# A fused attention and feed-forward kernel: the second part's second layer as seven block products, its weights streamed, its order from a list schedule

## The chip, the cores and the metric

The kernel runs on one core of a Trainium2 chip. TensorE (PE) multiplies matrices out of SBUF into PSUM, VectorE (DVE), ScalarE (ACT) and GpSimd (POOL) work on tiles, and SyncE (SP) issues most of the DMAs. Each engine runs its own instructions in order and waits on semaphores of the others. The metric is the time on the device in microseconds (us).

## The reference

It is attention over 4 batches, 8 heads, 768 tokens and heads of 64, followed by a feed-forward layer over the 3072 tokens:

```python
scores = scale * np.matmul(q, k.transpose(0, 1, 3, 2))
...                      # causal band of n_local and the first n_global keys, a bias by distance
a = a / (np.sum(a, axis=-1, keepdims=True) + 1e-09)
x = np.matmul(a, v)      # -> [3072, 512]
h = x @ w_in             # [512, 2048]
g = 0.5 * h * (1.0 + erf(h * inv_sqrt2))
out = (g @ w_out).astype(np.float32)      # [2048, 512]
```

The weights come as 64-bit words and are turned into 32-bit values on the chip. Each operand of a matmul is split into a high part and a low rest, so that one product takes three matmuls (high by high, high by low, low by high).

## The kernel before

The 2048 hidden columns are cut into 8 slices of 256, the tokens into 12 chunks of 256.

The first part does the attention of the 12 chunks and, for slices 0 to 2 (`NA`), both layers of each chunk (`m1`, `m2`, lines 508 to 551). It stores the partial sums (`store_partial`) and the chunks' x (`spill`). Meanwhile slices 3 to 7 are decoded (`stage_weights`, times in `DECODE`) and written to DRAM as high and low parts (`w1d`, `w2d`). A step is one chunk with one slice; START, EVENTS, SCALE and COPY say in which step and on which engine the attention's pieces are done.

The second part (`m1b`, `m2b`, lines 624 to 726) does slices 3 to 7 for 6 chunks of 512 tokens, 30 steps in all. There the first layer is already a scheme of seven block products in place of eight: the 256 columns by 512 rows of the weight slice are four blocks, x too, and sums of blocks (S1 to S4 of the weights, made when they are decoded; T1 to T4 of x, made in `fetch_x` and `make_x`) go into seven products of 6 matmuls of 128x256 each, so 42 matmuls a step (`product`, line 620). VectorE adds their results (line 629), ScalarE applies Gelu twice to each (a high part, and again the full value, from which VectorE takes the low rest, line 201). The second layer is done plainly: 4 groups of 6 matmuls of 128x512, 24 a step (`m2b`, line 722; the last step line 688), summed over the five slices in PSUM. At a chunk's end VectorE adds the partial sums of the first part (line 703), and they go out.

The five slices' weights for the second part are fetched once and stay in SBUF. GpSimd makes the sums of x. All first-part weights are read once more (`check_load`, `check_words`, line 314: 32 loads of 512 KB, 64 VectorE operations). The order within the second part is that of the code, moved about by the framework's scheduler.

Of the kernel before, what the change touches and what calls it, by code (L numbers as in the profile page):

```python
# [17 lines left out]
P = 128  # L18
# [21 lines left out]
EVS = {"load": (-3, -3, -2, -1), "s": (0, 0, 1, 1), "pt": (2, 2, 3, 3), "av": (3, 3, 4, 4)}  # L40
# [5 lines left out]
SCALE = ["vvvv", "vvvv", "gggg", "vvvv", "vvvv", "gggg", "vvvv", "gggg", "vvvv", "vvvv", "vvvv", "gggg"] + ["gggg"] * NP * (NCH - 3)  # L46
COPY = ["aavaaaaa", "aaaaaaaa", "avavvaaa", "vvvvvvvv"]
LOW = ["gvvg", "gvvv", "vvvv"]
PENS = "vvvvgggg"
GAP = 3  # L50
STEPS = [(c, s) for s in range(NA) for c in range(2)]
# [11 lines left out]
    18, 19, 20, 21,  # L63
    22, 23, 25, 27,
    27, 29, 29, 31))}
# [23 lines left out]
A11, A12, A22, S1, S2, S3, S4 = range(7)  # L89
B11, B21, B22, T1, T2, T3, T4 = range(7)  # L90
NEGMASK = -1000000000.0
# [23 lines left out]
class Fast:  # L115
    def __init__(self, tc, ctx, qT, kT, v, w, out, limits):
# [7 lines left out]
        self.stg = pool("stg", 2)  # L124
# [3 lines left out]
        self.gp = pool("gp", 3, stack=self.first)  # L128
        self.words = ExitStack()
# [10 lines left out]
        self.w1d = {s: tc.dram_tile([P, 2, 7, 256], F32, name=f"w1d{s}") for s in range(NA, NST)}  # L140
        self.w2d = {s: tc.dram_tile([P, 2, 2, DM], F32, name=f"w2d{s}") for s in range(NA, NST)}
# [9 lines left out]
        self.done, self.planned = set(), {}  # L151

    def consts(self):
# [6 lines left out]
        ta = self.stg.tile([P, 4, 256], F32, name="ta", tag="stage")  # L160
        tb = self.stg.tile([P, 4, 256], F32, name="tb", tag="stage")
# [53 lines left out]
    def load_weights(self, s, i):
        self.raw[s, i, "w"] = self.load_words(s, i, "w")
# [9 lines left out]
    def join_words(self, s, i):  # L226
# [3 lines left out]
        a = self.sm.tile([P, 512], I32, name=f"wb{s}_{i}", tag="o")  # L230
# [5 lines left out]
        if s >= NA and i < 2:  # L236
            af = self.sb.tile([P, 512], I32, name=f"wa{s}_{i}", tag="wa", bufs=2)
# [19 lines left out]
    def stage_weights(self, s, i):  # L257

        nc = self.nc
        if i == 0:  # L260
            self.w1s = self.sb.tile([P, 2, 7, 256], F32R, name=f"w1s{s}", tag="w1s")
            self.sums = self.sb.tile([P, 4, 256], F32, name=f"sums{s}", tag="sums")
        self.low_bits(s, i)
        self.join_words(s, i)
        af = self.af.pop((s, i))
        if i >= 2:
            w2 = self.sb.tile([P, 2, DM], F32R, name=f"w2s{s}_{i}", tag="w2s", bufs=2)
            self.his.append(nc.scalar.copy(w2[:, 0], af).ins)
            self.lo_dve(w2[:, 1], af, w2[:, 0])
            nc.sync.dma_start(self.w2d[s][:, :, i - 2, :], w2.bitcast(F32))  # L270
            return
        a = af.rearrange("p (d f q) -> p d f q", d=2, f=2)
        view = lambda x: x.rearrange("p b (d q) -> p d b q", d=2)
        hi, lo = self.w1s[:, 0], self.w1s[:, 1]
        if i == 0:
            self.a0 = a
            part, blocks = a[:, :, 0:1, :], slice(A11, A11 + 1)
        else:
            part, blocks = a, slice(A12, A22 + 1)
        h = nc.scalar.copy(view(hi[:, blocks]), part)  # L280
        self.his.append(h.ins)
        nc.vector.tensor_tensor(out=view(lo[:, blocks]), in0=part, in1=view(hi.bitcast(F32)[:, blocks]),
                                op=ALU.subtract)
        if i == 0:
            return
        add = lambda out, x, y, op: nc.gpsimd.tensor_tensor(out=out, in0=x, in1=y, op=op)
        sm = [self.sums[:, k].rearrange("p (d q) -> p d q", d=2) for k in range(4)]
        add(sm[0], self.a0[:, :, 1], a[:, :, 1], ALU.add)
        add(sm[1], sm[0], self.a0[:, :, 0], ALU.subtract)
        add(sm[2], self.a0[:, :, 0], self.a0[:, :, 1], ALU.subtract)  # L290
        add(sm[3], a[:, :, 0], sm[1], ALU.subtract)
        for k in range(4):
            ks, ss = slice(k, k + 1), slice(S1 + k, S1 + k + 1)
            nc.scalar.copy(hi[:, ss], self.sums[:, ks])
            self.lo_dve(lo[:, ss], self.sums[:, ks], hi[:, ss])
        nc.sync.dma_start(self.w1d[s], self.w1s.bitcast(F32))

    def fetch_w1(self, pool, s):
        self.w1[s] = pool.tile([P, 2, 7, 256], F32R, name=f"w1_{s}")
        self.nc.sync.dma_start(self.w1[s].bitcast(F32), self.w1d[s])  # L300

# [251 lines left out]
    def store_partial(self, t, k):  # L553
# [3 lines left out]
        o = self.sm.tile([P, DM], F32, name=f"o{c}_{k}", tag="o")  # L557
# [3 lines left out]
    def open_x(self):  # L561
        right = dict(side="right", reuse_waits="tile")
        self.wb = self.pool("wb", **right)
        self.xr = self.pool("xr", 2, **right)
        self.tf = self.pool("tf", **right)
        self.xcp = self.pool("xc", **right)

    def open_b(self):
        self.first.close()
        tile_waits = dict(reuse_waits="tile")  # L570
        self.gb = self.pool("gb", 2, **tile_waits)
        self.wb3 = self.pool("wb3", **tile_waits)
        self.pt = self.pool("part", 4, **tile_waits)

    def fetch_x(self, c):
        nc = self.nc
        xr = [self.xr.tile([P, 2, NP, CT], F32R, name=f"xr{n}{c}", tag=f"xr{n}") for n in "hl"]
        for j in range(2):
            for i in range(2):
                nc.sync.dma_start(xr[i].bitcast(F32)[:, j].rearrange("p d t -> p (d t)"), self.xd[2 * c + j][i])  # L580
        xs = self.tf.tile([P, 2, NP, CT], F32, name=f"xs{c}", tag="xs")
        for j in (1, 0):
            for i in (0, 1):
                ds = slice(2 * i, 2 * i + 2)
                nc.gpsimd.tensor_tensor(out=xs[:, j, ds], in0=xr[0].bitcast(F32)[:, j, ds],  # L585
                                        in1=xr[1].bitcast(F32)[:, j, ds], op=ALU.add)
        b = lambda i, j: xs[:, j, 2 * i:2 * i + 2, :]
        sub = lambda out, x, y: nc.gpsimd.tensor_tensor(out=out, in0=x, in1=y, op=ALU.subtract)
        tf = self.tf.tile([P, 2, 2, CT], F32, name=f"tf{c}", tag="tf")
        sub(tf[:, 0], b(0, 1), b(0, 0))  # L590
        sub(tf[:, 1], b(1, 1), b(0, 1))
        t2 = xs[:, 0, 0:2, :]
        sub(t2, b(1, 1), tf[:, 0])
        t4 = xs[:, 0, 2:4, :]
        sub(t4, b(1, 0), t2)
        self.xraw[c] = {T1: tf[:, 0], T2: t2, T3: tf[:, 1], T4: t4}
        for k, i, j in ((B11, 0, 0), (B21, 1, 0), (B22, 1, 1)):
            self.xc[c, k] = tuple(x[:, j, 2 * i:2 * i + 2, :] for x in xr)

    def make_x(self, c, k):  # L600
        if k < T1:
            return
        x = self.xraw[c][k]
        h, l = (self.xcp.tile([P, 2, CT], F32R, name=f"xc{n}{c}_{k}", tag=f"{n}{k}") for n in "hl")
        self.nc.scalar.copy(h, x)
        self.lo_dve(l, x, h)
        self.xc[c, k] = (h, l)

    def fetch_part(self, c):
        for k in range(4):  # L610
            self.part[c, k] = t = self.pt.tile([P, DM], F32, name=f"part{c}_{k}", tag="part")
            self.nc.sync.dma_start(t, self.pd[4 * c + k])

    def product(self, out, s, a, x, start, stop):
        h, l = x
        w = self.w1[NA + s]
        n = 0
        for d in range(2):
            for i, y in ((0, h), (0, l), (1, h)):
                self.nc.tensor.matmul(out, lhsT=w[:, i, a, d * P:(d + 1) * P], rhs=y[:, d, :],  # L620
                                      start=start and n == 0, stop=stop and n == 5, skip_group_check=not start)
                n += 1

    def m1b(self, t, half):
        nc = self.nc
        c, s = STEPS[t]
        c -= NCH
        mul = lambda out, a, b, start, stop: self.product(out, s, a, self.xc[c, b], start, stop)
# [454 lines left out]
```

## Time and profile before

| | us |
|---|---|
| median of 3 runs (679.25 to 679.66) | 679.28 |
| the profiled execution's own time | 679.46 |
| its span | 677.7 |
| first part, to the first matmul of the second | 354.9 |
| second part, to the end of the last matmul | 316.6 |
| after it | 6.2 |

The profile counts an engine as busy from an instruction's start to its end. Matmuls overlap in their pipeline, so the pace of TensorE is read from the starts of successive matmuls, not from their durations.

### The profile page before, as it was taken

The numbers are of one execution on the slowest core, as the hardware profiler recorded it, in microseconds if no ns is written. First come the engines' busy times: TensorE is split into PE (matmuls) and PEld (weight loads), VectorE is DVE, ScalarE is ACT, GpSimd is POOL, SyncE is SP. The second block draws the span as 40 slices with busy tenths as digits, with TensorE's granted clock in tenths as the row PEclk, the third lists the DMA queues.
The fourth block names the chain that finished last, engine by engine and source line by source line (L and its number), as shares of the span: only waits on it lengthen the run. The fifth ranks groups of instructions, "written<-read, shape, count | busy, mean of one in ns | idle before, by whom it ended". The sixth has DMA issues, their size and how long they took to land.

```text
span 677.7 us, 13212 instructions
## 1 busy us (share of the span) xinstructions
PE 667.2 (98%) x4809; PEld 591.4 (87%) x4809; DVE 434.9 (64%) x1194; ACT 361.4 (53%) x876; POOL 172.2 (25%) x243
## 2 busy tenths in 40 slices
PE   8999999999999999999999999999999999999996
PEld 7878888988888988888889899998999988899895
DVE  7999668977778878776136268559557535344333
ACT  5899678787787887875133142242332323332231
POOL 1140324244252522532146006006006005100000
PEclk9999999999999999999999999999999999999999
DMA  9678748979788796764499638348448105102101
GB/s 292 175 205 281 230 157 262 326 237 322 222 249 297 217 291 211 234 230 156 171 411 428 278 118 330 119 137 288 139 121 304 63 2 194 55 1 92 34 1 66
DMA packets 79785, 134.64 MB, mean 199 GB/s; under 512 B 15457, under 2 KB 51553, under 8 KB 77793
## 3 DMA queue, kind: packets, MB, share of 16 engines
q1 hardware_dynamic: 74992, 125.99, 55.6%
q10 hardware_dynamic: 4720, 7.74, 3.2%
q8 instruction: 40, 0.66, 0.4%
q14 instruction: 33, 0.26, 0.1%
HBM read 94.11 MB, written 39.58 MB: 197 GB/s over the span
## 4 chain that ended last, share of the span: by engine, by line


## 5 line engine op out<-in xcount | busy, mean ns | idle before, releaser
L722 PE MATMUL accb<-w,ghb 128*128 128x512 f32 x464 | 133.5, 391 | 0.0
L437 POOL TENSOR_SCALAR n<-n,su 128x256 f32<-128x256 f32 (+1 forms) x160 | 82.2, 534 | 164.1 <-DVE su L427 98.5
L722 PEld LDWEIGHTS accb<-w,ghb 128*128 128x128 f32 x464 | 84.3, 188 | 15.2
L421 ACT ACTIVATE n<-n,nmax 128x256 f32<-128x256 f32 (+1 forms) x192 | 91.8, 480 | 5.8 <-DVE nmax L405 5.3
L517 PE MATMUL h<-xh,winh 128*128 128x256 f32 x288 | 83.4, 290 | 0.0
L585 POOL TENSOR_TENSOR xs<-xrh,xrl 128x512 f32<-128x512 f32 x24 | 31.2, 1324 | 199.1 <-DVE glb L201 42.6
L517 PE MATMUL h<-xh,winl 128*128 128x256 f32 x288 | 81.6, 284 | 0.0
L517 PE MATMUL h<-xl,winh 128*128 128x256 f32 x288 | 81.4, 283 | 0.0
L722 PE MATMUL accb<-w,glb 128*128 128x512 f32 x232 | 79.5, 392 | 0.0
L405 DVE CUSTOM_DVE_ANT_0 n<-s,pens 128x256 f32<-128x256 f32 (+1 forms) x192 | 64.6, 396 | 3.1 <-PE s L382 2.8
L549 PE MATMUL acc<-wouth,gh 128*128 128x512 f32 x144 | 59.8, 417 | 0.0
L517 PEld LDWEIGHTS h<-xh,winh 128*128 128x128 f32 x288 | 54.9, 191 | 1.9 <-issue 0.5
L549 PE MATMUL acc<-woutl,gh 128*128 128x512 f32 x144 | 56.5, 394 | 0.0
L549 PE MATMUL acc<-wouth,gl 128*128 128x512 f32 x144 | 56.4, 397 | 0.0
L517 PEld LDWEIGHTS h<-xl,winh 128*128 128x128 f32 x288 | 55.0, 191 | 1.2
L644 ACT COPY p<-xy 128x256 f32<-128x256 f32 x30 | 11.1, 369 | 83.3 <-PE xy L620 83.1
L517 PEld LDWEIGHTS h<-xh,winl 128*128 128x128 f32 x288 | 54.9, 191 | 0.2 <-DVE wb L238 0.2
L620 PE MATMUL xy<-xrh,w 128*128 128x256 f32 x240 | 52.4, 282 | 1.0 <-DVE u L629 0.6
L620 PE MATMUL v<-xch,w 128*128 128x256 f32 x240 | 52.4, 281 | 0.0
L201 DVE TENSOR_TENSOR glb<-hs,ghb 128x256 fp32r<-128x256 f32 (+1 forms) x60 | 38.5, 644 | 18.2 <-ACT hs L674 14.7
L452 PE MATMUL t<-ident,n 128*128 128x128 f32 x352 | 48.2, 273 | 0.8 <-DVE n L437 0.5
L461 DVE COPY pt<-t 128x512 f32<-128x512 f32 (+1 forms) x76 | 45.5, 636 | 5.6 <-PE t L452 5.5
(127 smaller groups left out, 1497.7 us busy)
## 6 DMA issues: line engine op xcount, KB each, us to landing
w<-w SPq DMA_DIRECT2D x32, 512.0 KB, 4.8
c<-w SPq DMA_DIRECT2D x32, 512.0 KB, 4.5
w1d<-w1s SPq DMA_DIRECT2D x5, 1792.0 KB, 6.6
w<-w1d SPq DMA_DIRECT2D x5, 1792.0 KB, 16.9
kr<-kT SPq DMA_DIRECT2D x32, 224.0 KB, 4.4
pd<-o ACTq DMA_DIRECT2D x24, 256.0 KB, 4.0
part<-pd SPq DMA_DIRECT2D x24, 256.0 KB, 3.4
qr<-qT SPq DMA_DIRECT2D x45, 128.0 KB, 4.1
```

Source lines behind the costliest of these rows:

```text
L201: return self.nc.vector.tensor_tensor(out=out, in0=in_, in1=hi.bitcast(F32), op=ALU.subtract)
L405: ins = nc.vector.tensor_tensor_reduce(out=nn[:, j, :w], in0=sp[:, j, :w], in1=pen, scale=-0.125, scalar=3e38, op0=ALU.add, op1=ALU.min, a ...
L421: self.table(self.nc.scalar.activation(out=nn[:, j, :w], in_=nn[:, j, :w], func=AF.Exp, bias=mn[:, i:i + 1], scale=-1.0, accum_out=su[:, i ...
L437: ins = (nc.vector if vec else nc.gpsimd).tensor_scalar(out=nn[:, j, :w], in0=nn[:, j, :w], scalar1=su[:, i:i + 1], scalar2=0.0, op0=ALU.m ...
L452: nc.tensor.transpose(tp[:, i, :], nn[:, j, a * P:(a + 1) * P], self.ident)
L461: (nc.vector.tensor_copy if COPY[min(c, 3)][h] == "v" else nc.scalar.copy)(pt, tp[:, :n, :])
L517: nc.tensor.matmul(hp[:, f, :], lhsT=w[:, d, f * P:(f + 1) * P], rhs=x[:, d, :], start=n == 0, stop=n == 3 * NP - 1)
L549: nc.tensor.matmul(acc, lhsT=g[:, f, ks], rhs=w[:, f, :], start=s == 0 and n == 0, stop=s == NA - 1 and n == 5)
L585: nc.gpsimd.tensor_tensor(out=xs[:, j, ds], in0=xr[0].bitcast(F32)[:, j, ds], in1=xr[1].bitcast(F32)[:, j, ds], op=ALU.add)
L620: self.nc.tensor.matmul(out, lhsT=w[:, i, a, d * P:(d + 1) * P], rhs=y[:, d, :], start=start and n == 0, stop=stop and n == 5, skip_group_ ...
L644: nc.scalar.copy(p6, xy[:, 1])
L722: nc.tensor.matmul(acc, lhsT=g[:, f, ks], rhs=w[:, i, f, :], start=s == 0 and n == 0, stop=s == NB - 1 and n == 5)
```

## The change

The second layer of the second part becomes a scheme of seven products as well. The 512 tokens of a chunk are two halves q of 256, each with two blocks of 128 tokens; for each half and slice, g is four blocks of 128x128, `w_out`'s slice four of 128x256. Sums of g's blocks (`sum_g`, four VectorE operations) and their splitting into high and low (`split_g`) are made for each half, chunk and slice; sums of `w_out` when it is decoded. Each of the seven products takes 3 matmuls of 128x256 and has a region of PSUM of its own, summed over the five slices (`m2b`); only at the half's end are the seven combined (`post_sum`). Gelu is applied once to each value. The first layer's sums are partly made in PSUM: products accumulate into one bank, from which ScalarE copies the running sum (`first_copy`) and to which VectorE adds (`first_sum`). The first layer's weights are fetched anew for every step, in two pieces and two buffers (`fetch_w1`); the second layer's stay. Of the sums of x, only the first chunk's are still made on GpSimd. The check reads 64 loads of 256 KB.

The order of every engine in the second part comes from a list schedule: TensorE's order is written out, and an operation of another engine is placed when its inputs are there by assumed durations, by the due time that TensorE's order gives it; all engines are then held to that order. The last two groups of the first part's second layer (`n0`, `n1`) move into the second part's first step. In the first part, DECODE, the loads' times, SCALE (three of each chunk's first four scalings from GpSimd to VectorE) and COPY (two of eight copies a chunk from VectorE to ScalarE) change.

```diff
-COPY = ["aavaaaaa", "aaaaaaaa", "avavvaaa", "vvvvvvvv"]
...
+COPY = ["aavaaaaa", "aaaaaaaa", "avavvaaa", "vavvvvav"]
...
+    def fetch_w1(self, t, part):
+        s = STEPS[t][1]
+        cut = (slice(0, 4), slice(4, 7))[part]
+        n = cut.stop - cut.start
+        w = self.w1[t, part] = self.wb.tile([P, n, 2, 256], F32R, name=f"w1{'ab'[part]}_{t}", tag=f"w1{part}", bufs=2)
+        self.nc.sync.dma_start(w.bitcast(F32), self.w1d[NA + s][:, cut])
...
+        eng = self.nc.vector if c else self.nc.gpsimd
...
+        bank, a, b = {1: ("x", A11, B11), 6: ("x", S2, T2), 5: ("x", S1, T1), 3: ("x", S4, B22), 2: ("y", A12, B21),
+                      7: ("v", S3, T3), 4: ("v", A22, T4)}[k]
...
+        self.nc.scalar.copy(x, self.half[t]["x"])
...
+        self.nc.vector.tensor_tensor(out=x, in0=x, in1=self.half[t][bank], op=ALU.add)
...
+        a, b, op = ((g[:, G21], g[:, G22], ALU.add), (x[:, 0], g[:, G11], ALU.subtract),
+                    (g[:, G11], g[:, G21], ALU.subtract), (g[:, G12], x[:, 1], ALU.subtract))[k]
+        self.nc.vector.tensor_tensor(out=x[:, k], in0=a, in1=b, op=op)
...
+        dst, src = (slice(3, 7), self.gx[c, q, s]) if sums else (slice(0, 3), self.g[c, q, s][:, 1:4])
+        if low:
+            self.lo_dve(o[:, 1, dst], src, o[:, 0, dst])
+        else:
+            self.nc.scalar.copy(o[:, 0, dst], src)
...
+        for k in ks:
+            a, b = sides[k]
+            for n, (i, j) in enumerate(((0, 0), (0, 1), (1, 0))):
+                self.nc.tensor.matmul(out[k], lhsT=o[:, i, a], rhs=w[:, b, j],
+                                      start=s == 0 and n == 0 and k in (1, 4, 5, 6),
+                                      stop=s == NB - 1 and n == 2, skip_group_check=True)
...
+            gaps = (([(c, 0, s - 1, 0)], [(c, 0, s - 1, 1)], []) if c == 0 else (
+                ([(b, 0, 4, 0)], [(b, 0, 4, 1)], []), (both(b, 1, 0), both(b, 1, 1), both(b, 1, 2)),
+                (both(b, 1, 3), both(b, 1, 4), []), (both(c, 0, 0), both(c, 0, 1), []),
+                (both(c, 0, 2), both(c, 0, 3), []))[s])
...
+            pe += [(u, 1), (u, 2), (u, 7), (u, 6)] + gaps[0] + [(u, 5)] + gaps[1] + [(u, 3)] + gaps[2] + [(u, 4)]
```

TensorE, inside a step of the second part. In the order before, `accb` are the second layer's sums, `z` and `v` banks of the first layer:

```order
L722 MATMUL accb_0_5621<-w_4_4930,ghb_5635 128x512
L620 MATMUL v_5684<-xch_5_5378,w_5_4932 128x256
L620 MATMUL v_5684<-xcl_5_5379,w_5_4932 128x256
L620 MATMUL v_5684<-xch_5_5378,w_5_4932 128x256 x2
L620 MATMUL v_5684<-xcl_5_5379,w_5_4932 128x256
L620 MATMUL v_5684<-xch_5_5378,w_5_4932 128x256
L722 MATMUL accb_0_5621<-w_4_4930,ghb_5635 128x512
L722 MATMUL accb_0_5621<-w_4_4930,glb_5636 128x512
L722 MATMUL accb_0_5621<-w_4_4930,ghb_5635 128x512 x2
```

In the order now, `go` are the split blocks of g, `acc` the regions of the seven products, `x` and `v` banks of the first layer:

```order
L646 MATMUL x_8353<-xch_4_7658,w1a_8122 128x256
L703 MATMUL acc_8246<-w_5_5065,go_2_8292 128x256 x6
L703 MATMUL acc_8248<-w_5_5065,go_2_8292 128x256 x3
L703 MATMUL acc_8249<-w_5_5065,go_2_8292 128x256 x3
L703 MATMUL acc_8247<-w_5_5065,go_2_8292 128x256 x6
L703 MATMUL acc_8248<-w_5_5065,go_2_8292 128x256 x3
L646 MATMUL x_8353<-xch_3_7705,w1b_8235 128x256
```

A second layer of 24 matmuls 512 wide for 512 tokens has become 21 of 256 for each half, put between two products of the first layer.

VectorE, where a chunk's (now a half's) sums end. Before, `part` takes the sums of four groups, and nothing of the second layer is made by VectorE but `glb`:

```order
L201 TENSOR_TENSOR glb_6050<-xy_5992,ghb_6049 128x256
L703 TENSOR_TENSOR part_0_5548<-accb_0_5621,part_0_5548 128x512
L703 TENSOR_TENSOR part_1_5550<-accb_1_5628,part_1_5550 128x512
L629 TENSOR_TENSOR hs_5995<-u_49_5996,z_5993 128x256
L629 TENSOR_TENSOR hs_5995<-u_49_5996,v_5994 128x256
```

Now, `gx` are sums of g's blocks, `hc` sums of the first layer, `u`, `vw`, `r` and `part` belong to `post_sum`:

```order
L675 TENSOR_TENSOR gx_3_8596<-g_62_8264 128x128
L713 TENSOR_TENSOR part_3_8312<-part_3_8312,acc_8246 128x256
L675 TENSOR_TENSOR gx_3_8596<-g_62_8264,gx_3_8596 128x128
L713 TENSOR_TENSOR u_8612<-u_8612,acc_8246 128x256
L713 TENSOR_TENSOR part_3_8312<-part_3_8312,acc_8246 128x256
L713 TENSOR_TENSOR vw_8613<-u_8612,acc_8247 128x256 x2
L713 TENSOR_TENSOR r_8614<-vw_8613,acc_8247 128x256
L205 TENSOR_TENSOR go_1_8617<-g_60_7952,go_1_8617 128x384
L713 TENSOR_TENSOR vw_8613<-vw_8613,acc_8248 128x512
L322 SCALAR_TENSOR_TENSOR wand<-c_8610,wand 128x256
L205 TENSOR_TENSOR go_1_8617<-gx_1_8437,go_1_8617 128x512
L657 TENSOR_TENSOR hc_64_8563<-hc_64_8563,v_8533 128x256
```

The combination of seven products is a chain of VectorE operations, with the next half's operands (`go`) and sums of the first layer around it.

SyncE, at the start of the second part. Before, the weights of all five slices are fetched one after the other:

```order
L304 DMA w_4_4930<-w2d_157 128x2048
L300 DMA w_5_4932<-w1d_153 128x3584
L304 DMA w_5_4934<-w2d_158 128x2048
L300 DMA w_6_4936<-w1d_154 128x3584
L304 DMA w_6_4938<-w2d_159 128x2048
L300 DMA w_7_4940<-w1d_155 128x3584
L304 DMA w_7_4942<-w2d_160 128x2048
L206 DMA c_2_5132<-w 128x1024
```

Now `w1a` and `w1b` are a step's pieces of the first layer's weights, `c` the check's loads:

```order
L314 DMA w_4_5063<-w2d_157 128x3584
L314 DMA w_5_5065<-w2d_158 128x3584
L310 DMA w1a_5067<-w1d_153 128x2048
L310 DMA w1b_5070<-w1d_153 128x1536
L310 DMA w1a_5104<-w1d_154 128x2048
L314 DMA w_6_5131<-w2d_159 128x3584
L310 DMA w1b_5202<-w1d_154 128x1536
L310 DMA w1a_5225<-w1d_155 128x2048
L310 DMA w1b_5256<-w1d_155 128x1536
L314 DMA w_7_5287<-w2d_160 128x3584
L310 DMA w1a_5345<-w1d_151 128x2048
L318 DMA c_5389<-w 128x512
```

The second layer's weights are larger (3584 for 2048 words a row), and behind the fifth slice the first layer's begin again with the first, step after step.

## Rows read from the trace of the kernel before

**Rows 1.** The page, busy time, share of the span and instructions of each engine.
```profile
PE 667.2 (98%) x4809; PEld 591.4 (87%) x4809; DVE 434.9 (64%) x1194; ACT 361.4 (53%) x876; POOL 172.2 (25%) x243
```

**Rows 2.** Windows by stage; busy time of each engine, granted clock, DMA share, GB/s.
```profile
core 0: us, PE busy (x) PEld busy (x) DVE busy (x) ACT busy (x) POOL busy (x), PEclk, DMA share, GB/s
50.00:354.86 304.86, 304.86 (x2455) 267.43 (x2451) 222.31 (x664) 221.10 (x529) 103.44 (x176) 1.00 0.76 250
354.86:671.50 316.64, 315.57 (x1982) 284.70 (x1980) 168.58 (x359) 100.53 (x231) 54.70 (x40) 1.00 0.41 146
671.50:677.70 6.20, 0.00 (x0) 0.00 (x0) 0.77 (x3) 0.00 (x0) 0.00 (x0) 0.86 0.42 151
```

**Rows 3.** Timeline of TensorE where the second part begins; start, length.
```profile
354.62 0.40 PE L549 MATMUL acc<-wouth,gl 128*128 128x512 f32 x1
354.86 0.28 PE L620 MATMUL xy<-xch,w 128*128 128x256 f32 x1
...
364.93 1.55 PE L722 MATMUL accb<-w,ghb 128*128 128x512 f32 x6
366.32 0.40 PE L722 MATMUL accb<-w,glb 128*128 128x512 f32 x1
```

**Rows 4.** Timeline of TensorE, the last 24 matmuls.
```profile
665.86 0.63 PE L688 MATMUL accb<-w,ghb 128*128 128x512 f32 x2
...
671.08 0.39 PE L688 MATMUL accb<-w,glb 128*128 128x512 f32 x1
```

**Rows 5.** Groups by line, TensorE, second part; busy, mean ns, idle before.
```profile
L620 PE MATMUL xy<-xrh,w 128*128 128x256 f32 x240 | 52.4, 282 | 1.0 <-DVE u L629 0.6 <-ACT p L644 0.5
```

**Rows 6.** Timeline of VectorE in the second part.
```profile
389.23 0.42 DVE L629 TENSOR_TENSOR u<-p,xy 128x256 f32<-128x256 f32 x1 [4.72 <-PE xy L620]
389.68 0.42 DVE L629 TENSOR_TENSOR u<-u,z 128x256 f32<-128x256 f32 x1
...
395.95 0.42 DVE L629 TENSOR_TENSOR u<-p,xy 128x256 f32<-128x256 f32 x1
396.29 0.42 DVE L314 SCALAR_TENSOR_TENSOR wand<-c,wand 128x256 int32<-128x256 int32 x1
396.62 0.69 DVE L201 TENSOR_TENSOR xcl<-tf,xch 128x512 fp32r<-128x512 f32 x1
397.23 0.42 DVE L629 TENSOR_TENSOR u<-u,z 128x256 f32<-128x256 f32 x1
```

**Rows 7.** Groups by line, VectorE, second part.
```profile
L314 DVE SCALAR_TENSOR_TENSOR wand<-c,wand 128x256 int32<-128x256 int32 x64 | 34.7, 542 | 6.7 <-DMA c<-w 5.7
...
L201 DVE TENSOR_TENSOR glb<-hs,ghb 128x512 fp32r<-128x512 f32 x30 | 22.8, 760 | 14.7 <-ACT hs L674 14.7
```

**Rows 8.** Groups by line, GpSimd, second part.
```profile
L585 POOL TENSOR_TENSOR xs<-xrh,xrl 128x512 f32<-128x512 f32 x20 | 26.1, 1331 | 172.9 <-DVE glb L201 42.6 <-DVE u L629 41.8 <-DMA xrh<-xd8h 41.7
```

**Rows 9.** Groups by line, ScalarE, second part.
```profile
L673 ACT ACTIVATE ghb<-hs 128x512 fp32r<-128x512 f32 x30 | 18.6, 619 | 3.8 <-DVE hs L629 3.7
...
L644 ACT COPY p<-xy 128x256 f32<-128x256 f32 x30 | 11.1, 369 | 83.3 <-PE xy L620 83.1
```

**Rows 10.** Windows at the start of the second part, as in rows 2.
```profile
345.00:355.00 10.00, 10.00 (x54) 8.57 (x53) 4.43 (x5) 3.28 (x6) 4.83 (x4) 1.00 1.01 415
355.00:365.00 10.00, 10.00 (x86) 10.00 (x85) 5.27 (x12) 3.64 (x9) 8.03 (x7) 1.00 1.02 431
```

**Rows 11.** DMA issues by line; KB each, us from issue to landing.
```profile
w<-w1d SPq DMA_DIRECT2D x5, 1792.0 KB, 16.9
...
w<-w2d SPq DMA_DIRECT2D x5, 1024.0 KB, 13.3
```

**Rows 12.** Windows, the middle of the first part, as in rows 2.
```profile
100.00:310.00 210.00, 210.00 (x1749) 184.50 (x1748) 169.26 (x524) 168.59 (x413) 80.61 (x142) 1.00 0.80 255
```

**Rows 13.** Groups by line, copies of turned weights on ScalarE.
```profile
L461 ACT COPY pt<-t 128x512 f32<-128x512 f32 x13 | 7.2, 585 | 1.0 <-PE t L452 0.9
```

**Rows 14.** Timeline of the DMA issues of SyncE before the second part.
```profile
352.10 0.32 SPq L304 DMA_DIRECT2D w<-w2d  x1
```

More of the change, by code (lines that the diff above doesn't have):

```diff
@@ L128, in __init__ @@
         self.gp = pool("gp", 3, stack=self.first)
+        self.op = pool("op", 2, stack=self.first)
         self.words = ExitStack()
@@ L282, in stage_weights @@
         nc.vector.tensor_tensor(out=view(lo[:, blocks]), in0=part, in1=view(hi.bitcast(F32)[:, blocks]),
                                 op=ALU.subtract)
-        if i == 0:
+        if i % 2 == 0:
             return
[L286 to L289, printed above, removed]
@@ L581, in fetch_x @@
[L581 to L588, printed above, removed]
@@ L609, in fetch_part @@
[L609 to L617, printed above, removed]
+        x3 = [self.xr.tile([P, 6, CT], F32R, name=f"xr{n}{c}", tag=f"xr{n}") for n in "hl"]
+        x12 = [self.xr.tile([P, 2, CT], F32R, name=f"xo{n}{c}", tag=f"xo{n}", bufs=1) for n in "hl"]
@@ new lines, in make_x, with fetch_part @@
+    def make_x(self, c, k, low):
+        x = self.xraw[c][k]
+        if not low:
+            self.xc[c, k] = tuple(self.xcp.tile([P, 2, CT], F32R, name=f"xc{n}{c}_{k}", tag=f"{n}{k}") for n in "hl")
+            self.nc.scalar.copy(self.xc[c, k][0], x)
+        else:
+            self.lo_dve(self.xc[c, k][1], x, self.xc[c, k][0])
+    def fetch_part(self, c, q):
+        for a in range(2):
+            k = 2 * (1 - q) + a
+            self.part[c, q, a] = t = self.pt.tile([P, 2, 256], F32, name=f"part{c}_{k}", tag=f"part{a}")
+            self.nc.sync.dma_start(t.rearrange("p i e -> p (i e)"), self.pd[4 * c + k])
@@ L626, in m1b, with first_sum, gelu_b @@
+    def first_sum(self, t, k, bank):
+        x = self.half[t][f"c{k}"]
+        self.nc.vector.tensor_tensor(out=x, in0=x, in1=self.half[t][bank], op=ALU.add)
+    def gelu_b(self, t, q, f, src):
         c, s = STEPS[t]
         c -= NCH
-        mul = lambda out, a, b, start, stop: self.product(out, s, a, self.xc[c, b], start, stop)
-        add = lambda out, x, y: nc.vector.tensor_tensor(out=out, in0=x, in1=y, op=ALU.add)
-        last = s == NB - 1 and c + 1 < NBC
-        def done(k):
-            if last:
-                self.make_x(c + 1, k)
@@ L676, in m1b @@
-        self.g[t] = (gh, gl)
-    def last_m2b(self, t):
-        c, s = STEPS[t]
-        c -= NCH
-        gh, gl = self.g[t]
-        w = self.w2[NA + s]
-        prev = None
-        for f in range(2):
-            for k in range(4):
-                acc = self.acc[c, k, "b"]
-                for n, (g, i) in enumerate(((gh, 0), (gh, 1), (gl, 0))):
-                    ins = self.nc.tensor.matmul(acc, lhsT=g[:, f, k * P:(k + 1) * P], rhs=w[:, i, f, :], start=False,
-                                                stop=f == 1 and n == 2).ins
-                    if prev is not None:
-                        self.after(ins, prev, "the sums end one by one")
-                    prev = ins
-                if f == 1:
-                    self.store(c, k)
```

612 lines of the change are left out of this document (411 added, 201 removed).

## The prediction

> **What bounds the kernel now.** I read the page first, then windows by stage, then TensorE's timeline at both ends of the second part, then the groups of VectorE and ScalarE there. The page shows TensorE busy for 98% of the span and no other engine above 64%, its own weight loads apart [rows 1]. By stage, TensorE has no idle time the trace can show from 50 us to 354.86 us, and in the second part it is busy 315.57 of 316.64 us, at the full clock (granted 1.00, which is 2.4 GHz); 6.2 us follow its last matmul [rows 2]. So in the part that changes time goes as TensorE's instructions do, and everything else is cover, as long as it keeps up. The reader should take the pace of the matmuls from their starts. From 354.86 to 364.93 us stand the 84 matmuls of two steps' first layers, 256 wide: 10.07 us, 0.1199 each [rows 3]. Wide ones: the last 24 start between 665.86 and 671.08, 5.22/23 = 0.227 each [rows 4]; the six from 364.93 to 366.32 take 0.232 [rows 3]. The whole part agrees: it runs from 354.86 to 671.31 (the last start and 0.227), 316.45; less 1.07 idle and 1260 x 0.1199 = 151.1 this leaves 164.3 for its 720 wide matmuls, 0.228 each.
>
> **The change part by part.**
>
> *TensorE in the second part.* Away go 30 x 24 = 720 matmuls of 512 columns, 164.3 us. Added are 30 x 2 x 7 x 3 = 1260 of 256 columns, of the shape and type that the first layer has there; at 0.1199 that is 151.1 us. The first layer keeps its 1260. All of it is on the path that sets the end: -13.2 us. By 0.227 it would be -12.3, by 0.232 -15.9. Seven products in place of eight would give 12.5% of 164; the narrower matmul gives a third of that back, since two of 0.1199 cost more than one of 0.228.
> A rule speaks against this exchange. The Trainium skill ("TensorE: Matmul & The Clock Gate", section "Back-to-back issue gap") says that a stream of weight load and matmul is sustained at about 81 ns for 128 columns and 131 ns for 512. An estimate from that page, on the line between the two, is 98 ns for 256: the exchange would then cost 1260 x 98 - 720 x 131 ns, some 29 us more and not 13 less. The trace does not agree: this kernel's stream, with a weight load for each matmul, keeps 119.9 and 227 to 232 ns, and the measurement decides.
>
> *TensorE's waits.* Of the 1.07 us idle, 1.0 is ahead of first-layer products that wait for `u` and `p` [rows 5]; that scheme of sums is gone: -1.1. New waits come. A product that accumulates into bank x waits for ScalarE's copy of it: products 2 and 7 lie between, 12 x 0.12 = 1.44 us, against a drain of a matmul and a copy of 0.37 [rows 9]: covered, if the copy does not stand behind a split of 512 columns (0.62 [rows 9]). The last product into v waits for VectorE's `first_sum`; at the closest a second-layer piece and a product lie between, again more than its copy and addition. Behind a waiting matmul everything on TensorE is queued. At each half's end the seven sums must be combined before the next half's first matmul writes the same banks. There 36 matmuls of the first layer lie between, 4.3 us; the combination needs one ScalarE copy and eight VectorE operations. I work these out next.
>
> *VectorE.* Independent operations follow each other by 0.335 us for 256 columns (395.95, 396.29, 396.62) and 0.61 for 512; one that reads its predecessor's result follows by 0.45 [rows 6]. On the line between, 128 columns cost 0.20 and 384 0.47. For an interior chunk (five steps, 420 matmuls, 50.4 us of TensorE) VectorE gets: of 256 columns 15 `first_sum`, 18 of the combinations and 14 check words, 47 x 0.335 = 15.7; 40 `sum_g` x 0.20 = 8.0; 10 low parts of 384, 4.7; of 512 columns 10 low parts, 8 sums of x, 4 low parts of x and 2 in the combinations, 24 x 0.61 = 14.6. Sum 43.0 us, 85%. Before it was busy 168.58 of 316.64 us [rows 2], 53%. It is uneven: the second step of a chunk holds three halves' second layers (3 x 1.9), a combination (9 x 0.335 + 0.61 = 3.6), two sums of x (1.2), three sums (1.0) and check words (0.9), 12.4 us, against 105 matmuls, 12.6 us. The combination's own chain is about 3.0 us with perhaps 0.6 for dependent steps, inside the 4.3. Bounds for what the waits cost over 11 half-ends and 30 steps: nothing, if the operands made ahead (two halves' worth of buffers) carry VectorE through, and at the other end the rival below. I take 0.3 us at each of 11 half-ends, +3.3, near the lower end, since the independent pace is the row that most of these operations resemble.
> The eight sums of x for a chunk leave GpSimd, where one took 1.33 us [rows 8], and are in VectorE's list above. In exchange the slow moments go: check words average 0.54 us and the 512-column low parts 0.76 [rows 7], against 0.42 and 0.69 for single ones [rows 6]. I count no gain, as VectorE did not hold TensorE then.
>
> *ScalarE.* It had 100.5 us of work in the second part [rows 2]. Now a step has three copies and four Gelus of 256 columns and the high parts of two halves; even with full durations 7 x 0.37 + 2 x (0.50 + 0.62) = 4.8 us a step of 10. No term.
>
> *Transfers.* In chunk 0 a step is 63 matmuls, 7.55 us, and asks for a first-layer slice (1792 KB, 1.835 MB [rows 11]) and a second-layer slice, now of the same size, 486 GB/s; the trace gives 415 to 431 at full load [rows 10]. So chunk 0 lives on its head start: when the second part begins, x of two chunks, two steps of first-layer weights and one slice of second-layer weights are asked for. The buffers of the other second-layer slices come free as the first part's last steps end (352.10 before [rows 14]). From there 7 x 1.835 = 12.8 MB at 425 GB/s take 30 us, to 382; the fifth step starts at 354.9 + 7.8 + 3 x 7.55 = 385.3. Three us to spare: no term, with 0 and +7 as bounds. Later a step needs about 1.84 MB of weights, 0.4 of x, 0.55 of check words and 0.4 of partial sums and results in 10 us, 320 GB/s, and each piece of weights is asked for more than 10 us before its use. SyncE is in order, so a store that waits for a combination has the next weights behind it; ten us cover it.
>
> *The first part.* ScalarE is busy 168.6 of 210 us in its middle, VectorE 169.3 [rows 12]. ScalarE gets two copies of 0.585 [rows 13] a chunk of some 23 us and about 1 us more for each decoded slice, VectorE loses about as much as it gets. TensorE hides 85% as well as 80%, mostly: between -1 and +3, I take +0.5. `n0` and `n1` only change places with a first-layer product: 0.
>
> *The end.* Last product, one addition, a store: as before, 0 (6.2 us [rows 2]); bounds -0.5 and +0.5.
>
> Sum, against the profiled execution's own 679.46 us (the median of the runs is 679.28): 679.46 - 13.2 - 1.1 + 3.3 + 0.5 = 669.0 us.
>
> **The rivals.**
> 1. *VectorE becomes the bound (slower).* Place: the five interior chunks. If its operations follow each other as dependent ones do (0.115 more, over 121 of them), a chunk costs 56.9 us in place of 43.0 and TensorE's 50.4; by full durations (0.42, 0.29, 0.56, 0.69) it is 53.3. Halfway, 55.1, TensorE loses 4.7 us a chunk: 679.46 - 14.3 + 0.5 + 23.5 = 689 us, between 680 and 698. It decides from a mean pace 50.4/43.0 = 1.17 times the one I took, 0.39 for 256 columns. For it: 85% with uneven demand, and many operations that wait for ScalarE's high part. Against: independent ones are mixed in everywhere in the order, and GpSimd no longer works beside it.
> 2. *The weights of chunk 0 come late.* If the head start shrinks by ten us (SyncE held by a wait ahead of these loads), the fifth step waits 7 us: 676 us. For it: demand above the rate. Against: the loads need only the first part's last readers.
> 3. *The exchange gives nothing that shows:* waits of 14 us, spread. 679 us. Only by coincidence.
> 4. *No new waits at all,* the wide matmuls at the 0.232 end: 679.46 - 15.9 - 1.1 = 662.5 us.
>
> **How the numbers follow.** The forecast (669, own range 664 to 674) gets 0.62, rival 1 0.10, rival 2 0.10, rival 3 0.04, rival 4 0.14; the page's rule less than 0.01. A measurement of this kernel tells 0.2%, 1.4 us, from no change. Faster: 0.62 + 0.10 + 0.14 = 0.86; same 0.04; slower 0.10. The range from 662 to 677 takes in rivals 2 and 4 and leaves out rivals 1 and 3, the two that lie above it.
>
> **What would show it.** Pace: 256-wide matmuls of the second layer 0.118 to 0.121 apart, and the second part's matmuls over 302 to 306 us in place of 316.6. VectorE near 85% there, its 256-column additions about 0.34 apart; idle of TensorE named for `part`, `vw` or `go` at half-ends, 2 to 6 us in all. GpSimd nearly empty after the first chunk. The first part ends within 354 to 358 us. I am wrong if the pace of alternating banks is above 0.13, if idle of TensorE in the second part is over 10 us, if it stands in the first six steps ahead of a weight fetch, or if the first part grows by more than 3 us.

## The result, and the profile after

The changed kernel took 670.16 us (median of runs between 669.80 and 675.23) where the kernel before took 679.26: a ratio of 0.988, 95% interval 0.984 to 0.993. Faster was forecast, at 669.0. The profiled execution took 669.86, with a span of 668.1 (677.7 before), 9.6 less.

The page of the changed kernel, busy time, share of the span and instructions of each engine, as in [rows 1]:

```profile
PE 654.4 (98%) x5349; PEld 606.3 (91%) x5349; DVE 519.6 (78%) x1544; ACT 423.2 (63%) x1026; POOL 123.4 (18%) x201
```

Windows by stage, to be read against [rows 2]:

```profile
50.00:354.83 304.83, 302.86 (x2431) 264.60 (x2430) 222.77 (x670) 231.19 (x545) 103.22 (x169) 1.00 0.79 263
354.83:661.10 306.27, 305.08 (x2534) 303.07 (x2532) 251.24 (x701) 151.63 (x363) 5.26 (x4) 1.00 0.86 315
661.10:668.10 7.00, 0.12 (x2) 0.00 (x0) 1.73 (x4) 0.00 (x0) 0.79 (x2) 0.64 0.28 88
```

The second part starts where it did and ends 10 us earlier, with VectorE at 82% (53% before) and DMA at 0.86 (0.41). In the first part TensorE now has 2.0 us of idle, where it had none. The last stage grew from 6.2 us.

TensorE's timeline, second layer inside the stretch that holds the longest wait of the second part:

```profile
597.53 1.09 PE L703 MATMUL acc<-w,go 128*128 128x256 f32 x7
599.37 0.39 PE L646 MATMUL x<-xch,w1b 128*128 128x256 f32 x1 [0.76 <-ACT hc L653]
599.60 0.28 PE L646 MATMUL x<-xcl,w1b 128*128 128x256 f32 x1
599.71 0.39 PE L646 MATMUL x<-xch,w1b 128*128 128x256 f32 x2
599.94 0.28 PE L646 MATMUL x<-xcl,w1b 128*128 128x256 f32 x1
```

Undisturbed starts are 0.119 apart; the matmul behind a wait holds the next one off for 0.224 (599.37 to 599.60). So I count the *loss* of a second part: its length from the first product to the last matmul's end, less its narrow matmuls (1260 before, 2520 now, and the one that transposes the check's flag) at 0.1191 and the wide ones at 0.2285 (0.2294 in the kernel before, the mean of its 720). Before: 316.61 - 315.35 = 1.3 us. After: 306.40 - 302.99 = 3.4 us: four waits put off the next start by 1.8 us together, and the rest is matmuls held by up to 0.15 without an idle time that shows. The 302.99 holds 2.74 us for `n0` and `n1`, which stood in the first part before. The span's 9.6 us are then: exchange 720 x 0.2294 - 1260 x 0.1191 = -15.1; loss +2.1; first part +2.7 (it ends at the same time, without `n0` and `n1`); end +0.7.

What made VectorE wait in the second part, and its costliest groups there (busy, mean ns, idle before):

```profile
DVE wand L322 <- DMA c<-w: 20.9, 21, 3.1
DVE go L205 <- ACT go L689: 10.5, 10, 3.9
DVE gx L675 <- ACT g L665: 7.8, 5, 1.7
```

```profile
L205 DVE TENSOR_TENSOR go<-gx,go 128x512 fp32r<-128x512 f32 x60 | 42.0, 701 | 1.1 <-ACT go L689 1.0
L205 DVE TENSOR_TENSOR go<-g,go 128x384 fp32r<-128x384 f32 x60 | 33.1, 552 | 9.5 <-ACT go L689 9.4
...
L322 DVE SCALAR_TENSOR_TENSOR wand<-c,wand 128x256 int32<-128x256 int32 x64 | 27.0, 422 | 21.2 <-DMA c<-w 20.9
```

The check's loads (`c`) hold VectorE longest. VectorE's and ScalarE's timelines ahead of the wait at 599.37 show how that reaches TensorE:

```profile
595.97 0.43 DVE L322 SCALAR_TENSOR_TENSOR wand<-c,wand 128x256 int32<-128x256 int32 x1 [3.06 <-DMA c<-w]
596.32 0.48 DVE L675 TENSOR_TENSOR gx<-g 128x128 f32<-128x128 f32 x2
...
597.39 0.28 DVE L675 TENSOR_TENSOR gx<-g,gx 128x128 f32<-128x128 f32 x1
```

```profile
597.71 0.62 ACT L689 CAST go<-gx 128x512 fp32r<-128x512 f32 x1 [2.23 <-DVE gx L675]
598.64 0.42 ACT L665 ACTIVATE g<-hc 128x256 f32<-128x256 f32 x1 [0.31 <-DVE hc L657]
598.97 0.35 ACT L653 COPY hc<-x 128x256 f32<-128x256 f32 x1
```

VectorE stands 3.06 us for a load that nothing on TensorE needs; the sums `gx` come late behind it, ScalarE waits for them with its split, and the copy out of bank x, for which TensorE waits, stands behind the split and a Gelu. Why loads are late shows in their landing times and in windows along the second part (the columns of [rows 2]):

```profile
c<-w SPq DMA_DIRECT2D x64, 256.0 KB, 5.6
```

```profile
372.00:422.00 50.00, 50.00 (x420) 49.83 (x420) 38.17 (x106) 25.85 (x62) 0.00 (x0) 1.00 1.00 390
422.00:472.00 50.00, 49.76 (x416) 49.51 (x416) 44.88 (x124) 25.20 (x61) 0.00 (x0) 1.00 0.95 353
472.00:522.00 50.00, 50.00 (x420) 49.83 (x419) 44.80 (x124) 25.37 (x61) 0.00 (x0) 1.00 0.95 345
522.00:572.00 50.00, 50.00 (x422) 50.00 (x421) 43.67 (x122) 25.50 (x61) 0.00 (x0) 1.00 0.95 341
572.00:622.00 50.00, 49.18 (x411) 48.77 (x410) 41.82 (x125) 24.99 (x60) 0.00 (x0) 1.00 0.88 305
```

A load of 256 KB takes 5.6 us at the median to land, where the schedule assumes 2.5. In the middle three windows the DMA engines are busy 95% of the time at 341 to 353 GB/s. The longest wait falls into the last window (0.88): its load was issued at 588.35 and let VectorE go on at 595.97, and in between the share was 0.92, at 291 GB/s.

In the first part three groups of waits are new (the same view of before has none):

```profile
PE h L524 <- DVE gl L205: 0.7, 1, 0.7
PE t L459 <- POOL n L444: 0.6, 1, 0.6
PE h L524 <- DVE xl L205: 0.5, 2, 0.3
```

And at the end, VectorE and GpSimd after the last matmul's start at 660.94:

```profile
661.29 0.88 DVE L713 TENSOR_TENSOR part<-part,r 128x256 f32<-128x256 f32 x1
662.09 0.74 DVE L713 TENSOR_TENSOR part<-part,acc 128x256 f32<-128x256 f32 x2
```

```profile
661.16 0.73 POOL L741 TENSOR_TENSOR part<-part,vw 128x256 f32<-128x256 f32 x1
```

The sum beside GpSimd's takes 0.88 where its ten like take 0.42; before, VectorE ended 1.2 us after the last matmul's start, now 1.9, and 0.5 of the difference is that sum.

### The profile page after: what moved, and what is told of

It reads as the page before. It is cut to its first block, busy times and chain, and to the rows that moved or that the text cites. A ratio compares the mean times of both kernels' runs of the same rounds, so it can differ in the third digit from the quotient of the medians.

```text
span 668.1 us, 14962 instructions
## 1 busy us (share of the span) xinstructions
PE 654.4 (98%) x5349; PEld 606.3 (91%) x5349; DVE 519.6 (78%) x1544; ACT 423.2 (63%) x1026; POOL 123.4 (18%) x201
## 5 line engine op out<-in xcount | busy, mean ns | idle before, releaser
L703 PE MATMUL acc<-w,go 128*128 128x256 f32 x1260 | 161.5, 282 | 0.2
L703 PEld LDWEIGHTS acc<-w,go 128*128 128x128 f32 x1260 | 155.0, 190 | 0.9 <-DVE go L205 0.5
L444 POOL TENSOR_SCALAR n<-n,su 128x256 f32<-128x256 f32 (+1 forms) x133 | 66.9, 521 | 167.3 <-DVE su L434 78.2
L665 ACT ACTIVATE g<-hc 128x256 f32<-128x256 f32 x90 | 36.9, 418 | 52.6 <-DVE hc L657 52.3
L653 ACT COPY hc<-x 128x256 f32<-128x256 f32 x90 | 33.1, 368 | 42.9 <-PE x L646 42.5
L205 DVE TENSOR_TENSOR gl<-h,gh 128x512 fp32r<-128x512 f32 x36 | 24.8, 688 | 33.5 <-ACT h L534 33.3
L689 ACT CAST go<-g 128x384 fp32r<-128x384 f32 x60 | 30.6, 512 | 30.5 <-PE acc L703 29.9
L487 PEld LDWEIGHTS av<-pt,vr 128*64 128x64 f32 x704 | 39.0, 137 | 9.5 <-issue 3.3
L487 PE MATMUL av<-pt,vr 128*64 128x128 f32 x704 | 46.8, 277 | 0.4
```

The costliest lines, as they stand in the source:

```text
L205: return self.nc.vector.tensor_tensor(out=out, in0=in_, in1=hi.bitcast(F32), op=ALU.subtract)
L444: ins = (nc.vector if vec else nc.gpsimd).tensor_scalar(out=nn[:, j, :w], in0=nn[:, j, :w], scalar1=su[:, i:i + 1], scalar2=0.0, op0=ALU.m ...
L487: ins = nc.tensor.matmul(av[64 * hh:64 * hh + 64, j, :], lhsT=vt[hh][:, vi, :], rhs=pt[hh][:, i, :], start=(j, a) == js[0], stop=(j, a) == ...
L653: self.nc.scalar.copy(x, self.half[t]["x"])
L665: self.table(self.nc.scalar.activation(out=out, in_=self.half[t][src], func=AF.Gelu))
L689: self.nc.scalar.copy(o[:, 0, dst], src)
```

## The experiments

Each is the changed kernel with one edit, timed against the kernel before on one chip. Durations that the list schedule assumes are changed with the edit where they belong to it (e1, e2, e5). "Start" is the end of the first part's work (where first-part matmuls stand behind the second part's first product, at 0.2285 each, they are counted back); loss as above. Both are read from one execution each, and executions differ: the four of the changed kernel took 669.80 to 675.23. In e1, e2, e5 and e8 to e11 the traces have the first part's instructions of TensorE, VectorE and ScalarE in the changed kernel's order, and yet start lies between 355.1 and 356.5. A difference in start below 1.7 us is therefore no finding.

| run | us, median | ratio, 95% interval | start | loss |
|---|---|---|---|---|
| changed kernel | 670.16 | 0.988 (0.984 to 0.993) | 354.8 | 3.4 |
| e1_wide | 690.11 | 1.016 (1.014 to 1.017) | 355.8 | 8.6 |
| e2_check_twice | 682.27 | 1.004 (1.003 to 1.005) | 355.5 | 14.1 |
| e8_no_check | 667.23 | 0.982 (0.980 to 0.983) | 355.1 | 0.9 |
| e9_check_no_load | 668.80 | 0.984 (0.982 to 0.986) | 355.1 | 1.4 |
| e10_check_ahead | 688.77 | 1.013 (1.011 to 1.015) | 355.2 | 19.7 |
| e11_check_ahead_4us | 676.55 | 0.996 (0.995 to 0.998) | 355.1 | 9.8 |
| e5_x_on_gpsimd | 687.48 | 1.012 (1.009 to 1.014) | 356.5 | 20.3 |
| e6_framework_order | 681.74 | 1.004 (1.002 to 1.005) | 355.7 | 12.2 |
| e3_tables_back | 674.40 | 0.992 (0.990 to 0.994) | 360.9 | 4.9 |
| e7_w2_sums_on_vector | 673.44 | 0.990 (0.988 to 0.992) | 356.5 | 6.9 |
| e4_no_w2_sums | 676.74 | 0.996 (0.994 to 0.998) | 357.5 | 7.5 |
| e12_no_w2_sums_one_store | 674.49 | 0.994 (0.992 to 0.995) | 356.2 | 5.4 |

**The exchange.**

```diff
-                self.nc.tensor.matmul(out[k], lhsT=o[:, i, a], rhs=w[:, b, j], ...)   # 7 products, 256 wide
+                self.nc.tensor.matmul(wide[k], lhsT=o[:, i, a], rhs=w[:, b:b + 2, j], ...)   # k in 1, 4, 6, 7
```

> The changed kernel with only the exchange of the second layer's matmuls undone: for each half, chunk and slice 12 matmuls of 512 columns in place of 21 of 256 (into the same four banks, so the output is not the reference's); every other engine does what it does in the changed kernel. Theory, the gain is the exchange on TensorE's path: 720 wide ones at 0.227 to 0.232 for 1260 at 0.12, so 12 to 16 us more than the changed kernel's 670.2, 682 to 686 us, above the kernel before. Rival, the gain comes from the other parts (Gelu once, order by a list schedule, sums in PSUM) and TensorE has slack for the rest: within 4 us of 670.

690.11 us, 20 above the changed kernel and above the theory's range too. The paces give 14.5 of it (720 x 0.2285 less 1260 x 0.1191), the loss 5.2 more; the undisturbed wide matmuls of this run stand 0.230 apart, which moves 1.3 us of that loss to the pace. With the exchange undone and the rest left in, the kernel is slower than before: the exchange is where the gain comes from.

**How much room VectorE has, and what the check's loads cost.**

```diff
-        self.behind(self.nc.vector.scalar_tensor_tensor(out=self.wand, ...))
+        for _ in range(2):
+            self.behind(self.nc.vector.scalar_tensor_tensor(out=self.wand, ...))
```

> The changed kernel with each of the 64 check operations of VectorE done twice (64 more of 256 columns, some 21 to 27 us of VectorE work over steps 5 to 27 of the second part; the list schedule knows of it). Theory, VectorE has slack behind TensorE: less than 5 us more, 670 to 675. Rival, VectorE is by now as near the bound as TensorE: most of its 21 us appear, 685 to 692 us.

682.27 us: 12 above, between the two theories. The profile has VectorE at 277.25 of 317.10 us, 87%, and the loss grew by 10.7 us for 26.0 us of added work. VectorE's slack is neither whole nor gone: of what was added here 40% shows.

```diff
-                dma(("cl", n), lambda n=n: self.check_load(n), ...)
-                op(("cw", n), "DVE", dve(256), lambda n=n: self.check_words(n), ...)
```

> Leaves out the check of the weights' words in the second layer's part of the run: its 64 loads of 256 KB (16.8 MB) and its 64 VectorE operations (27 us of VectorE at 0.422 us each). TensorE's work is untouched. Theory: TensorE's own work sets the second part (2.3 us of visible stalls in 306), so the check hides almost wholly: 668 to 670 us. Rival: transfers (0.95 of the queues' time) and VectorE (82%) cost TensorE more than the visible gaps, by later operands everywhere: 658 to 664 us.

For the next run, the loads alone are gone:

```diff
-                dma(("cl", n), lambda n=n: self.check_load(n), ...)
+                if n == 0:
+                    dma(("cl", n), lambda n=n: self.check_load(n), ...)
```

> Leaves out 63 of the check's 64 loads; all 64 VectorE operations stay, on the one tile that was loaded. Beside the run without any check it tells VectorE's time from the transfers. Theory: the 2.3 us of stalls in the second part come from check loads that land late (20.9 us of VectorE's waits name them), not from VectorE's work: 667.5 to 669.5 us, as without the check. Rival: it is VectorE's 27 us of operations that delay the operands: no gain, 669.5 to 670.5 us, and only the run without any check gains.

667.23 us is 0.8 below the theory's interval and 3 above the rival's; 668.80 is inside the theory's. The intervals of the ratios overlap, so the traces must tell the two apart: the loss is 3.4 with loads and operations, 1.4 with the operations alone, 0.9 with neither. VectorE is as busy without the loads as with them (253 and 251 us), so of the 2.1 us that the loss grew over the kernel before, 2.0 go with the loads in these traces. The runs agree: the slowest of e9's four (669.23) is below the fastest of the changed kernel's four (669.80), and the kernel before took 679.26 beside both. (Another 1.5 us between the profiled executions of e9 and e8 lie behind the last matmul, 8.2 and 6.7 us; why is open.) Windows of e9 over the second part:

```profile
354.90:659.00 304.10, 303.94 (x2533) 302.56 (x2532) 253.47 (x700) 151.77 (x363) 4.82 (x4) 1.00 0.74 263
```

**Loads asked for earlier.** The loads' spacing, the schedule's landing time and the time by which a load is due (6 us earlier, in a line left out here) are changed together:

```diff
-        op(name, "SP", kb / 380, fn, deps, 2.5, due)
+        op(name, "SP", kb / 380, fn, deps, 7.0 if name[0] == "cl" else 2.5, due)
-        checks = [4 + n * 23 // 64 for n in range(64)]
+        checks = [2 + n * 26 // 64 for n in range(64)]
```

> All work stays. The list schedule is told that a check's load takes 7.0 us to land instead of 2.5 (5.6 us at the median in the profile), and the 64 loads are spread from step 2 on at 64 over 26 steps instead of from step 4 at 64 over 23. Theory: VectorE no longer waits for these loads (20.9 us in 21 waits), and the second part loses its 2 us of stalls: 667.5 to 669.5 us. Rival: with two buffers for the loads the waits only move: 669.5 to 671 us.

Then 4.0 in place of 7.0, `2 + n * 23 // 64`, and due 3 us earlier:

> All work stays. The check's loads are scheduled with 4.0 us to land (2.5 in the changed kernel, 7.0 in the run before, where the last checks and with them the flag's reduction came 83 places later on VectorE and TensorE waited 13 us for it), and they begin at step 2 instead of 4, at the old spacing. Theory: VectorE waits less for loads than its 20.9 us, the flag is early, and the second part comes near that of the run without the loads: 668 to 669.5 us. Rival: with two buffers the loads stay late, or the moved VectorE work makes other waits: 669.5 to 672 us.

688.77 and 676.55 us: neither theory nor rival saw this. VectorE's waits for these loads did shrink, from 20.9 us to 5.2 and 8.1, and two other waits took their place. In e10 the last checks come later in the schedule, the kernel's flag needs them all, and its transposition stands in TensorE's order ahead of the last half:

```profile
PE flag_ps L1141 <- DVE bad L1137: 13.0, 1, 13.0
```

In e11 the earlier loads stand ahead of the fifth slice of second-layer weights in SyncE's queue: that fetch is issued at 392.72 (378.43 in the changed kernel), and TensorE's timeline shows

```profile
396.25 0.28 PE L646 MATMUL x<-xch,w1a 128*128 128x256 f32 x1
402.25 1.01 PE L703 MATMUL acc<-w,go 128*128 128x256 f32 x3 [5.72 <-DMA w<-w2d]
```

Behind it the granted clock (the column ahead of the last two) is 0.50, the lower level (1.2 GHz), until about 407:

```profile
396.00:402.25 6.25, 0.53 (x6) 0.33 (x4) 3.93 (x15) 1.21 (x3) 0.00 (x0) 0.85 0.89 351
402.25:404.00 1.75, 1.75 (x8) 1.75 (x9) 0.43 (x1) 0.00 (x0) 0.00 (x0) 0.50 0.96 382
404.00:406.00 2.00, 2.00 (x11) 2.00 (x11) 0.00 (x0) 0.15 (x1) 0.00 (x0) 0.50 1.05 420
406.00:408.00 2.00, 2.00 (x14) 2.00 (x13) 0.76 (x2) 0.65 (x2) 0.00 (x0) 0.69 0.97 401
408.00:410.00 2.00, 2.00 (x19) 2.00 (x18) 1.43 (x3) 1.58 (x4) 0.00 (x0) 1.00 0.68 239
```

So the 5.7 us cost about 8: 21 matmuls at 0.213 add 2.0. No version in which the check is left whole beat the changed kernel.

**Who makes the sums of x, and the schedule's order.**

```diff
-        eng = self.nc.vector if c else self.nc.gpsimd
+        eng = self.nc.gpsimd
```

> All work stays; the sums of the first layer's operands in the second part are made on GpSimd for every chunk (1.33 us each before), as in the kernel before, instead of VectorE (0.70 us each). Theory: VectorE loses 17 us of its work, but its operations beside GpSimd take longer (the check 0.542 us beside it, 0.422 now), which gives most of that back; GpSimd's chain of eight sums (11 us) still fits into a chunk: 668 to 671 us. Rival: VectorE's load sets the stalls, and 17 us less of it is worth a microsecond or more: 666.5 to 668 us.

687.48 us: both wrong. GpSimd at work stretches VectorE's operations. VectorE's groups from 526 to 538 us, where GpSimd makes eight sums (526 to 537.4) and TensorE then waits 3.1 us:

```profile
L205 DVE TENSOR_TENSOR go<-gx,go 128x512 fp32r<-128x512 f32 x2 | 3.3, 1672 | 0.0
L322 DVE SCALAR_TENSOR_TENSOR wand<-c,wand 128x256 int32<-128x256 int32 x2 | 2.9, 1445 | 2.2 <-DMA c<-w 2.1
L205 DVE TENSOR_TENSOR go<-g,go 128x384 fp32r<-128x384 f32 x1 | 1.6, 1625 | 0.0
L713 DVE TENSOR_TENSOR part<-part,acc 128x256 f32<-128x256 f32 x2 | 0.8, 410 | 0.0
L657 DVE TENSOR_TENSOR hc<-hc,v 128x256 f32<-128x256 f32 x2 | 0.8, 410 | 0.0
```

These `go` and `wand` take 2.4 to 3.4 times their means of 701, 422 and 552 ns in the changed kernel; `part` and `hc`, of whose operands one lies in PSUM, keep their 0.41. GpSimd's sums take 1.3 to 1.6 us each. The Trainium skill ("SBUF — State Buffer", section "SBUF: two separate sides") says that VectorE, with two operands in SBUF, and GpSimd take turns at a pair of ports, an instruction at a time. The trace agrees: each such operation of VectorE lasts about as long as one of GpSimd's. TensorE's waits name VectorE: 9.1 us in four for `hc`, 2.8 for `go` and `vw`. After the longest of them the clock falls too (45 matmuls of this run are 0.213 apart).

```diff
-            self.in_order(traced[k:], True)
```

> All work stays; the second part's instructions are not held in the list schedule's order on each engine, but left to the order in which the framework's own priorities put them. Theory: the order written by the schedule is worth much here, since VectorE has little slack and a chunk's sums would come before the operands that TensorE waits for: 675 to 690 us. Rival: the emission order already is the schedule's, and holding it adds nothing: 668 to 673 us.

681.74 us: the theory's size, by another cause. It is SyncE, not VectorE: four fetches of partial sums stand ahead of the next weights and wait. SyncE's queue and TensorE's wait:

```profile
373.74 9.39 SPq L627 DMA_DIRECT2D part<-pd  x4
383.47 0.32 SPq L310 DMA_DIRECT2D w1a<-w1d  x1
```

```profile
PE x L646 <- DMA w1a<-w1d: 9.1, 1, 9.1
```

**The first part's 2.7 us.** Tables of times and engines set back; sums of second-layer weights on VectorE; those sums left out, with three stores, then with one:

```diff
-EVS = {"load": (-3, -3, -1, -1), ...}
+EVS = {"load": (-3, -3, -2, -1), ...}      # e3; SCALE, COPY and DECODE too
```

> The changed kernel with the first part's tables (load times, SCALE, COPY, DECODE) as before. The first part cost 2.7 us more in the changed kernel. Theory, the added decoding work of the second layer's sums on GpSimd and ScalarE is what costs, and the tables make room for it: without them GpSimd has three more scalings a chunk, so the same or 1 to 4 us slower, 670 to 674. Rival, the tables themselves cost the 2.7 us: 667 to 668 us.

```diff
-            add(sm[0], a0[:, 1], a0[:, 0])      # and three more, in e7 with nc.vector
+            for k, n in ((0, 3), (3, 3), (6, 1)):      # e4
+                nc.sync.dma_start(self.w2d[s][:, k:k + n], self.wst.bitcast(F32)[:, 0:n])
+            nc.sync.dma_start(self.w2d[s], self.wst.bitcast(F32)[:, 0:1].to_broadcast([P, 7, 2, 256]))      # e12
+            return
```

> The changed kernel without the sums of the second layer's weights in the first part (four GpSimd subtractions, two ScalarE copies and two VectorE operations a slice are left out, the same bytes are stored, so the output is not the reference's). Theory, these sums are the first part's 2.7 us: the first matmul of the second part comes 2 to 3 us earlier and the time is 667 to 668 us. Rival, the tables or the transfers cost it: 670 us.

> The four sums of weight blocks of the second layer's slices, made in the first part, run on VectorE instead of GpSimd (20 operations of 0.3 to 0.6 us instead of 1.3). Theory: the first part's 2.7 us come from VectorE's and ScalarE's new operations there and from GpSimd only in small part (one wait of 0.6 us names it): 669 to 671 us. Rival: GpSimd's sums are what is late and slow VectorE beside them: 667 to 669 us.

> Leaves out the four sums of weight blocks, and their split, for each of the five slices of the second layer in the first part (20 GpSimd sums, 10 ScalarE copies, 10 VectorE subtractions); one DMA of the same size still fills the scratch, with one block written seven times, so the output is not the reference's. Theory: these operations are what the first part lost: the second part begins near 352 us instead of 354.8 and the time is 666.5 to 668.5 us. Rival: the first part's loss is from its other edits (the order, the first layer's sums): it still begins at 354.5 us or later, and the time is 669 to 671 us.

The tables earn their place: with the old ones the first part ends 6.1 us later in the profiled execution, the slowest of its four (by the medians the kernel is 4.2 slower). With the weight sums on VectorE the first part ends 1.7 us later, no more than in e5, whose first part is the changed kernel's; so that is not shown to be the sums. The 673.44 us are above theory and rival, mostly for a larger loss later. Without the sums it should have ended sooner and did not: at 357.5 in e4, of which 2.85 us are a wait made by my three stores, and at 356.2 in e12, of which 1.1 us are a new wait of TensorE for VectorE. Less these it is 354.7 and 355.1, against 354.8. Both times, 676.74 and 674.49, lie above theory and rival. The 352 of my theory is reached in neither, so it fell: nothing here shows that the sums are what the first part lost. But leaving them out also moves other instructions (24 more matmuls of the first part come behind the second part's first product in e12), and the spread of starts is 1.7 us, so a cost below that is not excluded. Of the three new waits the one for `n` stands in e4 and e12 too, with 0.7 us, so the sums do not make that one. Which edit makes them stays open, and so does why the loss is larger in e3, e4, e7 and e12 (4.9 to 7.5); the changed kernel's own run of 675.23 shows that executions can differ by as much.

## Why the prediction was right

- *The exchange, -13.2: right, a little small.* It is -15.1, inside the bounds of -12.3 to -15.9: the narrow pace became 0.1191, not 0.1199, and the wide one before was 0.2294 in the mean. The estimate from the figures of the Trainium skill ("TensorE: Matmul & The Clock Gate", section "Back-to-back issue gap"), 29 us more, is refuted: narrow matmuls stay at 0.119.
- *Idle gone and new waits, -1.1 + 3.3: right in size by luck, wrong in place.* The loss went from 1.3 to 3.4, so +2.1 for my +2.2. But I put it at the half-ends, and TensorE waits for the combination only once, at the very end (0.13 us for `u`, and as long in e8 and e9): e9 shows that the growth goes with the check's loads. The place was in my text as a condition: the copy out of bank x is covered "if the copy does not stand behind a split of 512 columns". At 598.97 it does, since the split waited for VectorE.
- *VectorE at 85%: right (82%).* Rival 1 did not come. In e2, at 87%, the loss is 14.1; in e5 the time is in rival 1's range, by stretches in which GpSimd slows VectorE. (By full durations rival 1's chunk is 53.5, not 53.3, which changes nothing.)
- *Transfers, no term: the step that failed.* The rate was near (320 forecast, 305 to 353 in the four windows from 422 to 622), but I took from it that "ten us cover it". The engines are 88 to 95% busy at it, and the smallest transfers, which VectorE takes in order, land late; that the one makes the other is argued, not tested apart. For the weights of chunk 0 I had 3 us to spare. The fifth slice is asked for at 378.43, such a fetch lands after some 10, and it is first used at 395.75: about 7. Rival 2 is real all the same: e11 made it by moving the small loads ahead.
- *The first part, +0.5 with -1 to +3: +2.7,* near the upper bound, of which 2.0 is idle, in waits on VectorE and GpSimd that [rows 12] did not show; the sums of second-layer weights, on which I put it afterwards, are not shown to be the cause.
- *The end, 0 within 0.5: +0.7,* outside its bounds, 0.5 of it a sum on VectorE beside one on GpSimd.

The errors, -1.9 (exchange), +2.2 and +0.7, nearly cancel: 669.0 forecast, 670.16 measured. The direction and its cause, the exchange, were foreseen; that the number is so close is luck.

## What to carry to other kernels

Price an exchange of matmul shapes by start-to-start paces in the same kernel. Then look, on each in-order engine, for the wait that is of no use to TensorE, such as a small load whose result is needed much later: what stands behind it pays. In e10 and e11 a longer landing time in the planner did not mend it: the small loads that moved forward put a large one back (e11), and checks that came later held up the flag (e10).

## What the runs showed of the hardware

- After a wait TensorE may run at the lower level for a while: 5.7 us of idle in e11 were followed by 21 matmuls at 0.213, 3.1 us in e5 by a granted clock of 0.50 from 537 to 540. It is not the length of the one wait alone: 2.5 us that ended at 591.28 in e5 were followed by 0.50, 2.85 us that ended at 145.86 in e4 by 1.00.
- The first matmul after a wait holds the next for 0.224 in place of 0.119, even after a wait of 0.76 us or less.
- VectorE's operations on two SBUF operands take up to 3.4 times as long while GpSimd works (`wand` 1.45 for 0.422 us in e5), those with one in PSUM no longer (0.41).
- DMA engines can be 95% busy at 345 GB/s, where [rows 10] has 415 to 431 at full load: the rate alone doesn't show what is free.
